# Three more of the zero fills written in rows of 56 KB, in a decode step with its gradients

## The chip, the cores and the metric

The kernel runs on one core of a Trainium2 chip. The metric is device time in microseconds, measured by whole runs; the profile comes from one further execution that the hardware profiler recorded.

## What is computed

One decode step of attention over a cached window, gated by a small dense network, and the gradients of all inputs:

```python
# x: (2, 1, 512); k_cache, v_cache: (2, 8, 32768, 128); wq: (512, 4096); wo: (4096, 512)
W = min(4096, max(256, Sk // 4))                    # 4096
k = repeat(k_cache[:, :, Sk - W:, :], rep); v = repeat(v_cache[:, :, Sk - W:, :], rep)
p = softmax(einsum("bhqd,bhkd->bhqk", q, k) * Dh ** -0.5)
s = einsum("bhqk,bhkd->bhqd", p, v) -> rows @ wo
g = silu((relu(xn @ w1 + b1) ** 2) @ w2 + b2)       # xn = layernorm(x)
out = x + s * g
# returned: out and the gradients by x, k_cache, v_cache, wq, wo, w1, b1, w2, b2
```

Only the last 4096 of the 32,768 cached positions take part. So the gradients by k_cache (out_2) and v_cache (out_3), 134 MB each in bfloat16, are computed in their last eighth and are zero in the other seven eighths. Writing these zeros is most of what the kernel moves: 32 blocks (2 tensors x 2 batch rows x 8 heads) of 28,672 rows of 128 bfloat16 values, 7.34 MB each.

## The kernel before

**The fills.** Each of the 32 blocks of zeros is one "fill". Fills 0 to 30 (the loop at L118 to L123; 0 to 15 go to out_2, 16 to 30 to out_3) are issued at the start of the program by GpSimd, on the software DMA queue; fill 31 comes at the very end from SyncE (L641). The source is the tile `zt` (L80, L81): 128 partitions of 14,336 zero bytes, set once by VectorE. The function `zf` (L90 to L102) issues one DMA: `nent` partitions, each writing `rows` cache rows of 256 bytes in one piece, repeated `rep` times. The source is bytes and the destination is wider, so the DMA widens each byte as it goes: with up to 112 rows (`ZG`) to a piece the destination counts as bfloat16 and 14,336 source bytes become 28,672; above that (L95 to L97) it counts as 32-bit float and the same 14,336 source bytes become 57,344.

There are three forms of fill:

- long (`zlong`, L107): one instruction, 128 pieces of 224 rows, 57,344 bytes (56 KB) each;
- undivided but not long: one instruction, 128 pieces of 112 rows, 28,672 bytes (28 KB), twice. These are fills 0, 1, 9, 14 and 21;
- divided (`zshort`, L108 to L117): fills 2, 4, 6, 8, 10, 13, 15 and 20, in four or five instructions of different piece sizes, down to single rows of 256 bytes.

Together they are 58 instructions. GpSimd may have eight of them outstanding: the first eight start at once and each later one waits until the one eight before it has landed (each of eight semaphores serves every eighth fill). GpSimd does hardly anything else, only one small store in the last round (L512).

**The computation.** It runs in four rounds (L430), each of one batch row and four heads. A round needs the V window and the K window, 4 MB each, which SyncE loads (`load`, L215 to L218) in packets of 32 KB into one buffer for V and one for K. TensorE transposes V in groups and multiplies (`scores`, L378 to L392), then K, then the softmax and its gradient follow on ScalarE and VectorE. `outer_store` (L412 to L422) then writes the gradient by V over the V buffer itself and ScalarE stores it to out_3; only when that store has landed may SyncE load the next round's V (L543). K goes the same way (L548, L550). So within a round the stores and loads of one buffer follow each other strictly, and the transfers share the 16 DMA engines with the fills.

**The end.** In the last round the remaining gradients are computed; ScalarE stores wq's and wo's (L581, L587), SyncE stores w2's (out_8, L610), the gradient by x (L634) and w1's (out_6, L636). Behind these, on SyncE, stands fill 31 (L641), in pieces of 14,336 bytes; it is kept behind the out_6 store and also waits until fill 29, the last but one of the software queue, has landed (L642).

Of the kernel before, what the change touches and what calls it, by code (L numbers as in the profile page):

```python
# [16 lines left out]
def kernel(  # L17
# [86 lines left out]
    ZQ = 2 * B * HKV  # L104
    zparts = [(out_2, q) for q in range(B * HKV)] + [(out_3, q) for q in range(B * HKV)]

    zlong = (3, 5, 7, 11, 12, 16, 17, 18, 19, 22, 23, 24, 25, 26, 27, 28, 29, 30)  # L107
    zshort = {  # L108
        2: ((5, 8, 2), (120, 68, 3), (128, 32, 1), (16, 1, 1)),
        4: ((3, 1, 2), (2, 99, 6), (128, 112, 1), (128, 102, 1), (86, 1, 1)),  # L110
# [561 lines left out]
```

## Time and profile before

| | us |
|---|---|
| median of 3 runs | 766.2 (766.17 to 766.35) |
| the profiled execution | 766.29 |
| its span | 764.5 |
| PE busy | 399.7 (52%) |
| DVE busy | 275.8 (36%) |
| ACT busy | 214.5 (28%) |
| GpSimd busy | 35.1 (5%) |

| moved | |
|---|---|
| written to HBM | 280.50 MB |
| read from HBM | 45.62 MB |
| mean rate over the span | 427 GB/s |
| DMA packets | 12,473 |

The span runs from the first to the last instruction of the program; the execution's own time adds what lies around it. Engines: PE is TensorE's matmuls, DVE VectorE, ACT ScalarE, POOL GpSimd, SP SyncE. A DMA is counted from its issue to its landing; its bytes travel as packets on one of the queues (q0 the software queue, q1 SyncE's, q10 ScalarE's), and all queues share 16 DMA engines. One contiguous piece of a fill is one packet: the records of single packets show 2304 of 57,344 bytes and 2176 of 28,672 on q0. The page shows the span in 40 equal slices; a digit is the busy share of a slice in tenths. The chain of waits is the work that ended last, followed back from the last instruction.

### The profile page before, as it was taken

To read this page: it belongs to the slowest core of one execution; us is meant where nothing else is said; L and a number is where in the kernel's file an instruction comes from. 1 tells how busy PE (TensorE), PEld (TensorE's weight loads), DVE (VectorE), ACT (ScalarE), POOL (GpSimd) and SP (SyncE) were. 2 spreads that over 40 slices of the span, in tenths; PEclk is the share of its full clock that TensorE was granted. 3 is DMA by queue.
4 is the path that set the end of the run, shared out by engine and by line. 5 is a ranking of instruction groups with operands and counts; after the bars stand their busy time and mean duration, and the time that the engine had idled before them with its cause. 6 is when DMAs were issued, how large, how long until landed. Compare 5 with 4: busy or idle time off the path is not lost.

```text
span 764.5 us, 9399 instructions
## 1 busy us (share of the span) xinstructions
PE 399.7 (52%) x4118; PEld 261.8 (34%) x4118; DVE 275.8 (36%) x483; ACT 214.5 (28%) x313; POOL 35.1 (5%) x67
## 2 busy tenths in 40 slices
PE   0166774848503766870486683017645938759100
PEld 0153363734102654430275430016543424232000
DVE  3034252355501346450254653003343515567100
ACT  0034441145500124560122553002142307316100
POOL 3000010010000000000000000000000000000000
PEclk9998898968755995785599577559876957555555
DMA  9999999999999999999999999999999999999998
GB/s 360 433 425 427 442 422 430 438 426 425 429 428 438 427 446 430 413 427 435 435 427 440 427 433 438 420 433 429 437 430 436 430 440 430 418 438 425 436 417 379
DMA packets 12473, 326.73 MB, mean 427 GB/s; under 512 B 2898, under 2 KB 2906, under 8 KB 2934
## 3 DMA queue, kind: packets, MB, share of 16 engines
q0 software_dynamic: 8000, 227.55, 70.4%
q1 hardware_dynamic: 2696, 56.63, 19.3%
q10 hardware_dynamic: 1736, 41.95, 13.5%
q8 instruction: 32, 0.52, 0.3%
q14 instruction: 9, 0.07, 0.0%
HBM read 45.62 MB, written 280.50 MB: 427 GB/s over the span
## 4 chain that ended last, share of the span: by engine, by line
PE 33%; DMA 32%; DVE 14%; ACT 7%; issue 6%; ACTq 0%; DVEq 0%; SPq 0%
DMA out_dram<-nat 13%; DMA nat<-in_A_v_cache_dram 8%; DMA nat<-in_A_k_cache_dram 8%; PE ov L418 5%; PE s_ps L391 4%; PE tp L384 4%; DMA b_bf<-in_B_b_dram 4%; DVE tring L159 3%; PE dp_ps L391 2%; ACT p_bf L452 2%; ACT nat L157 2%; DVE ds_bf L465 2%; DVE nat L159 2%; PE wps L585 2%; PE ps L407 1%
## 5 line engine op out<-in xcount | busy, mean ns | idle before, releaser
L384 PE MATMUL tp<-pperm,nat 128*128 128x128 bf16 x1024 | 81.9, 228 | 136.4 <-DMA nat<-in_A_v_cache_dram 117.3
L159 DVE COPY tring<-tp 128x1024 bf16<-128x1024 bf16 (+1 forms) x98 | 65.5, 689 | 177.9 <-PE tp L384 168.3
L384 PEld LDWEIGHTS <-nat 128*128 128x128 bf16 x1024 | 70.8, 102 | 142.9 <-DMA nat<-in_A_v_cache_dram 119.3
L157 ACT CAST nat<-ov 128x512 bf16<-128x512 f32 x160 | 87.4, 590 | 61.9 <-PE ov L418 61.2
L157 ACT COPY tring<-tp 128x1024 bf16<-128x1024 bf16 (+1 forms) x34 | 34.4, 1011 | 239.7 <-PE tp L384 223.1
L159 DVE CAST nat<-ov 128x512 bf16<-128x512 f32 x96 | 65.7, 690 | 54.1 <-PE ov L418 51.4
L391 PEld LDWEIGHTS <-zz 128*128 128x128 bf16 x512 | 49.6, 100 | 37.3 <-issue 31.3
L101 POOL DMA_DIRECT2D out_dram<-zt x58 | 33.5, 581 | 529.3 <-DMA out_dram<-zt 526.1
L418 PE MATMUL ov<-bd,ds_bf 128*128 128x512 bf16 x128 | 49.2, 459 | 5.6 <-DVE nat L159 3.7
L418 PE MATMUL ov<-bd,p_bf 128*128 128x512 bf16 x128 | 48.6, 452 | 4.3 <-DVE nat L159 1.4
L391 PE MATMUL dp_ps<-tring,zz 128*128 128x256 bf16 x256 | 39.2, 284 | 12.1 <-DVE tring L159 6.9
L391 PE MATMUL s_ps<-tring,zz 128*128 128x256 bf16 x256 | 39.0, 275 | 10.9 <-DVE tring L159 9.9
L407 PE MATMUL ps<-t,nat 128*128 128x16 bf16 x1024 | 29.0, 174 | 13.7 <-DVE bd L372 6.8
L407 PEld LDWEIGHTS <-nat 128*128 128x128 bf16 x1024 | 28.9, 104 | 16.6 <-issue 11.4
L159 DVE CAST wq<-wps 128x512 bf16<-128x512 f32 x16 | 11.0, 690 | 42.4 <-PE wps L578 42.2
L399 PE MATMUL tp<-ident_bf,p_bf 128*128 128x128 bf16 x64 | 7.5, 312 | 34.9 <-ACT p_bf L452 34.9
L452 ACT ACTIVATE p_bf<-e_sb,rl 32x512 bf16<-32x512 f32 x16 | 22.8, 1424 | 3.4 <-DVE rl L449 3.3
L157 ACT CAST wq<-wps 128x512 bf16<-128x512 f32 x16 | 9.3, 586 | 50.6 <-PE wps L578 50.6
L465 DVE SCALAR_TENSOR_TENSOR ds_bf<-dp_ps,delta,p_bf 32x512 bf16<-32x512 f32 x16 | 21.8, 1360 | 0.2
L418 PEld LDWEIGHTS <-ds_bf 128*128 128x128 bf16 x128 | 12.9, 107 | 20.5 <-issue 18.2
L418 PEld LDWEIGHTS <-p_bf 128*128 128x128 bf16 x128 | 12.7, 108 | 19.5 <-issue 16.4
L399 PEld LDWEIGHTS <-p_bf 128*128 128x128 bf16 x64 | 6.5, 145 | 36.0 <-ACT p_bf L452 36.0
(195 smaller groups left out, 437.6 us busy)
## 6 DMA issues: line engine op xcount, KB each, us to landing
out_dram<-zt POOLq DMA_DIRECT2D x23, 7168.0 KB, 101.3
out_dram<-nat ACTq DMA_DIRECT2D x8, 4096.0 KB, 41.4
out_dram<-zt POOLq DMA_DIRECT2D x7, 3584.0 KB, 63.4
nat<-in_A_v_cache_dram SPq DMA_DIRECT2D x4, 4096.0 KB, 32.6
nat<-in_A_k_cache_dram SPq DMA_DIRECT2D x4, 4096.0 KB, 27.3
out_dram<-zt SPq DMA_DIRECT2D x1, 7168.0 KB, 52.2
out_dram<-zt POOLq DMA_DIRECT2D x2, 3488.0 KB, 64.6
out_dram<-zt POOLq DMA_DIRECT2D x1, 6120.0 KB, 85.8
```

The source lines that it names most:

```text
L101: sw_fill.append(nc.gpsimd.dma_start(out=v, in_=zs))
L157: nc.scalar.copy(out=out_ap, in_=in_ap)
L159: nc.vector.tensor_copy(out=out_ap, in_=in_ap)
L384: nc.tensor.transpose(tp[:, j, :], nat[:, g * CC + half * CH + j, :], pperm[:].rearrange("p b k -> p (b k)"))
L391: nc.tensor.matmul(out_ps[:, half * CH * PB:(half + 1) * CH * PB], lhsT=zbuf[:, pr, o:o + R], rhs=tT[:, :, pr, :], start=(g == 0 and pr == ...
L399: nc.tensor.transpose(tp[:, cc, :], src[:, half * CH + cc].rearrange("r k b -> r (k b)"), ident_bf[:, :])
L407: nc.tensor.matmul(ps[:], lhsT=nat[:, g * CC + half * CH + cc, :], rhs=cols[half][:, cc, :, g, :], start=(half == 0 and g == 0 and cc == 0 ...
L418: nc.tensor.matmul(ov[:], lhsT=src[:, cc].rearrange("r k b -> r (k b)"), rhs=bd[:, gh * 4:(gh + 1) * 4, :], start=True, stop=True)
L452: nc.scalar.activation(out=p_bf[rb, :, :, pr], in_=e_sb[rb], func=ACT.Copy, scale=rl[rb, 0:1])
L465: nc.vector.scalar_tensor_tensor(out=ds_bf[rb, :, :, pr], in0=dp_c[rb], scalar=delta[rb, 0:1], in1=p_bf[rb, :, :, pr], op0=ALU.subtract, o ...
L585: nc.tensor.matmul(wps[:], lhsT=o_rows[:, j:N:NJ], rhs=ds_rows[:, :], start=True, stop=True)
```

## The change

Fills 9, 14 and 21 are added to the list of long fills. Their one instruction each then writes 128 pieces of 57,344 bytes in place of twice 128 pieces of 28,672 bytes. The bytes, the number and order of the instructions, the source tile and all waits stay. Fills 0 and 1 keep pieces of 28,672 bytes.

```diff
-    zlong = (3, 5, 7, 11, 12, 16, 17, 18, 19, 22, 23, 24, 25, 26, 27, 28, 29, 30)
+    zlong = (3, 5, 7, 9, 11, 12, 14, 16, 17, 18, 19, 21, 22, 23, 24, 25, 26, 27, 28, 29, 30)
...
     for qi in range(ZQ - 1):
         r = 0
         whole = (P, ZR // P, 1) if qi in zlong else (P, ZG, ZR // (P * ZG))
         for n, rows, rep in zshort.get(qi, (whole,)):
             r = zf(*zparts[qi], r, n, rows, rep)
```

## The prediction, made before the result

> **What bounds the kernel now.** I read the page's slices first, because a kernel that mostly moves bytes shows there whether its transfers or its chain of waits set the end.
>
> ```profile
> DMA  9999999999999999999999999999999999999998
> GB/s 360 433 425 427 442 422 430 438 426 425 429 428 438 427 446 430 413 427 435 435 427 440 427 433 438 420 433 429 437 430 436 430 440 430 418 438 425 436 417 379
> ...
> q0 software_dynamic: 8000, 227.55, 70.4%
> q1 hardware_dynamic: 2696, 56.63, 19.3%
> q10 hardware_dynamic: 1736, 41.95, 13.5%
> ```
>
> The reader is to see that no slice is below nine tenths but the last, and that the rate stays near 430 GB/s whatever the engines compute. q0 is the software queue (the fills), q1 holds SyncE's transfers, q10 ScalarE's. PE is busy for 52% of the span, so it is not the bound. The DMA engines are: 326.73 MB at 430 GB/s need 760 us of the 764.5.
>
> Next the stretches around the fills concerned and at the end (columns: stretch, length, five engines' busy time, clock, DMA share, GB/s):
>
> ```profile
> 530.30:547.10 16.80, 9.95 (x107) 8.51 (x105) 3.71 (x6) 2.02 (x2) 0.54 (x2) 0.80 1.10 454
> 547.10:564.00 16.90, 11.09 (x130) 9.30 (x127) 7.36 (x15) 4.44 (x6) 0.53 (x2) 1.00 1.01 429
> ...
> 711.40:743.40 32.00, 0.00 (x0) 0.00 (x0) 0.00 (x0) 0.00 (x0) 0.00 (x0) 0.50 0.99 423
> 743.40:760.80 17.40, 0.00 (x0) 0.00 (x0) 0.00 (x0) 0.00 (x0) 0.00 (x0) 0.50 1.00 430
> 760.80:764.50 3.70, 0.00 (x0) 0.00 (x0) 0.00 (x0) 0.00 (x0) 0.00 (x0) 0.50 0.37 159
> ```
>
> From 711.4 on nothing computes, and the transfers still need 52 us at full rate. The last row is the only loose end: 0.59 MB in 3.7 us, so the 16 engines do not stop together.
>
> Third, GpSimd in order of time. Each fill instruction waits for the one eight before it (eight start at once, later ones one by one), so its start marks a landing. With fill 9 the 24th fill instruction, fill 14 the 36th and fill 21 the 49th, these rows give the time in which each was moved: fill 9 from 239.5 to 266.1, fill 14 from 363.2 to 384.8, fill 21 from 530.3 to 547.1. Fills 18 and 22 (56 KB rows) are 440.5 to 457.4 and 547.1 to 564.0.
>
> ```profile
> 239.51 0.59 POOL L101 DMA_DIRECT2D out_dram<-zt  x1 [5.83 <-DMA out_dram<-zt]
> 266.05 1.14 POOL L101 DMA_DIRECT2D out_dram<-zt  x2 [25.95 <-DMA out_dram<-zt]
> ...
> 363.18 0.53 POOL L101 DMA_DIRECT2D out_dram<-zt  x1 [14.38 <-DMA out_dram<-zt]
> 384.77 0.53 POOL L101 DMA_DIRECT2D out_dram<-zt  x1 [21.06 <-DMA out_dram<-zt]
> ...
> 440.46 0.55 POOL L101 DMA_DIRECT2D out_dram<-zt  x1 [16.19 <-DMA out_dram<-zt]
> 457.36 0.53 POOL L101 DMA_DIRECT2D out_dram<-zt  x1 [16.35 <-DMA out_dram<-zt]
> ...
> 530.27 0.53 POOL L101 DMA_DIRECT2D out_dram<-zt  x1 [0.93 <-DMA out_dram<-zt]
> 547.07 0.53 POOL L101 DMA_DIRECT2D out_dram<-zt  x1 [16.26 <-DMA out_dram<-zt]
> 563.98 0.53 POOL L101 DMA_DIRECT2D out_dram<-zt  x1 [16.38 <-DMA out_dram<-zt]
> ```
>
> Last, who shares the engines with fill 9. Between 248 and 256 us the DMA view has a load of K (32 KB packets) beside it:
>
> ```profile
> q1 hardware_dynamic: 57, 1.87, 54.8%
> q0 software_dynamic: 55, 1.58, 46.3%
> ```
>
> As many packets of one queue as of the other, so the bytes divide as the packet sizes do.
>
> **What the Trainium skill says.** "DMA: Bandwidth & Descriptors", section "Queues, rings and completion order", says that an engine goes round-robin over the queue rows that have work, a packet at a time. The 57 to 55 above agrees, and a row of a fill counts there as one packet. The same page, "Issuing engines are not separate DMA queues": transfers from all issuers share the same 16 engines; the constant rate agrees. Its section "Where 436 GB/s comes from" puts the ceiling at 435.2 GB/s; the trace holds 429 to 433 over long stretches. "Why small descriptors are slow" names a fixed cost of about three cycles per packet; the packet records here show a few ns (below).
>
> **The change part by part.** 3 fills x 256 rows of 28 KB go, 3 x 128 rows of 56 KB come. The 58 fill instructions, their order, their waits and their bytes stay, and nothing moves on any engine or past any other queue.
>
> (a) *The packets themselves.* In the packet records a 28,672-byte row takes 1.079 us on its engine, a 57,344-byte row 2.153 us: 2 x 1.079 - 2.153 = 0.005 us less for each long row. Each engine gets 384 / 16 = 24 of them: -0.12 us. The landings say the opposite, but little: fill 21 (28 KB rows, almost alone) took 16.80 us, fills 18 and 22 (56 KB rows) 16.90 and 16.91: +0.11 each, +0.33 for three. That interval starts and ends with the engine that is furthest behind, so I trust the records more: I take -0.1 and keep -0.12 to +0.33.
>
> (b) *Loads beside these fills.* A hardware packet of 32 KB now waits for a row of 56 KB: one turn is 1.06 us longer (28,672 B at 27.1 B/ns, the rate of a long fill on one engine: 7.34 MB / 16 / 16.9 us). The K load of round 1 lies inside fill 9 (issued 236.6, landed after 25.8 us, at 262.4). It has 128 / 16 = 8 packets an engine, so it lands up to 8 x 1.06 = 8.5 us later. TensorE reaches its K transposes near 264, so some 1.5 us is free and up to 7 passes to the chain. Fill 14 lies beside the end of round 2's V load and most of its K load (issued 369.5): 118 packets of q1 move there, 7.4 an engine, up to 8 us. Fill 21 now sees only the last packets of round 3's K load, for which TensorE waits 5.03 us at 540.5; if that load comes later, all of it falls there, up to 8.5. Lower end: 2 us in all. Upper: 7 + 8 + 8.5 = 23.5. I take 12.
>
> (c) *What such a delay costs.* Its cover is the fills still queued. While a load or a store is late, its engine time goes to rows of later fills, so the total work and the rate are kept. At the end: of the 13.52 MB in 711.4 to 743.4, 6.48 are fills and 4.26 ScalarE's stores (DMA view of that stretch). Only out_8, out_6 and the last fill (1.84 + 1.84 + 7.34 MB) hang on SyncE's last issues at 704.2, 710.8 and 711.4. So with these late the engines still have 10.74 MB, or 25 us, and another 4 us from out_8, which is issued 7 us ahead. A chain that is 29 us late costs nothing; 12 us costs nothing. The last fill also waits for fill 29's landing (711.3 by its semaphore), which comes earlier, not later, when the chain slips.
>
> (d) *The issue side.* GpSimd's 0.53 us per fill is off the path: the last fill instruction issues at 564 and lands at 742.
>
> Sum: -0.1 + 0 + 0. The profiled execution took 766.29 us, 1.8 more than its span; it stands 0.1 above the median, so the forecast in medians is 766.1.
>
> **The rivals.**
>
> *Slower: the chain slips beyond its cover.* The three fills have 3 x 8 long turns an engine, so 25.4 us at most is lost directly in them. But with a slip, round 3's loads also slide from fill 20 (28 KB rows and 56 short ones) into fills 21 to 23, 8 turns x 1.06 = 8.5 us more. That makes 34, and it decides from 29 on: +5 us, 771. For it: these loads do lie on the chain (the K load's 32.2 us at 508.25 is one of its long pieces). Against it: every packet would have to be hit, and the slack of round 1 counts off. 0.11.
>
> *The loose end grows.* The engines' last packets end between 760.9 and 763.2 us. If the long rows shift which engine is behind by one or two packets of the last fill (0.53 us each), the end moves by 0.5 to 1: 767.1. For it: the end is set by one engine alone. Against it: each engine gets the same share of these rows. 0.14.
>
> *Faster: fewer switches pay.* Fills 9 and 14 move at 431 to 432 GB/s beside loads, the long rows of 564 to 614 at 433. If all 65 us gained that 0.4%, it would be -0.3, and engines that stop together would give 1.0 more: 764.9; two packets beyond that pass the bound. 0.06 for anything below it.
>
> *The rows are cut again.* If a 56 KB row went out as two packets, nothing would change: 766.2. The records of the other long fills show single packets of 57,344 bytes, so I give it nothing apart.
>
> **How the numbers follow.** 0.69 for the forecast, the rest as above (of the loose end 0.03 lies past the bound). What this kernel's measurement tells from no change is put at 0.2%, 1.5 us: 764.7 to 767.7. The forecast and nearly all of the loose end lie inside: 0.80 within, 0.14 slower, 0.06 faster. The range leaves those two out and spans (a) with half a loose end below and a whole one above: 765.2 to 767.6.
>
> **What would show it.** q0 should have 7,616 packets; the K load of round 1 should land 28 to 34 us after its issue; SyncE's last issue should move from 711 to 715 to 735, with the software queue done before 743; the DMA row should stay at nine tenths to the last slice. I am wrong if the DMA share drops after 735 because the last fill is issued too late, if one engine runs on alone at the end, or if the rate inside the three fills falls.

## The result, and the profile after

The changed kernel is slower: 825.3 us median (805.0 to 834.1 in 6 runs) against 766.3 (766.1 to 767.4), a ratio of 1.060 with a 95% interval of 1.053 to 1.068. The ratio leaves out runs more than 1.5% above the fastest of their kernel (three of the six), and the profile below is of such a run, at 834.05 us, with a span of 832.3. Experiment 9 has the profile of a shorter run of nearly the same kernel.

The page's slices of the profile after, with the chain by line:

```profile
DMA  9999999999999999999999999999999994147179
GB/s 360 434 432 419 439 424 445 419 438 422 433 430 429 446 428 428 424 434 438 428 434 428 424 445 426 433 433 421 448 423 437 435 436 189 76 180 303 51 334 397
...
q0 software_dynamic: 7616, 227.55, 64.6%
...
DMA nat<-in_A_k_cache_dram 21%; DMA out_dram<-nat 15%; PE ov L418 5%; PE s_ps L391 4%; DMA b_bf<-in_B_b_dram 4%; PE tp L384 3%; ACT p_bf L452 2%; ACT nat L157 2%; DVE tring L159 2%; DVE ds_bf L465 2%; DVE nat L159 2%; PE wps L585 1%; PE ps L407 1%; PE dops L312 1%
```

The change did what it says: 7616 packets in place of 8000, for the same bytes. Up to slice 33 the engines move as much as before. Then there is a hole: the fills are used up, and the engines wait for the computation. Loads of K stand at 21% of the chain now. Before they stood at 8%:

```profile
DMA out_dram<-nat 13%; DMA nat<-in_A_v_cache_dram 8%; DMA nat<-in_A_k_cache_dram 8%; PE ov L418 5%; PE s_ps L391 4%; PE tp L384 4%; DMA b_bf<-in_B_b_dram 4%; DVE tring L159 3%; PE dp_ps L391 2%; ACT p_bf L452 2%; ACT nat L157 2%; DVE ds_bf L465 2%; DVE nat L159 2%; PE wps L585 2%; PE ps L407 1%
```

The hole in stretches (columns as in the prediction: stretch, length, busy time of five engines, clock, DMA share, GB/s):

```profile
698.00:714.00 16.00, 15.79 (x89) 7.04 (x89) 6.20 (x16) 4.74 (x9) 0.00 (x0) 0.89 0.00 1
714.00:801.00 87.00, 68.73 (x539) 33.41 (x539) 52.79 (x84) 36.79 (x64) 0.50 (x1) 0.59 0.41 176
801.00:809.00 8.00, 6.45 (x16) 1.80 (x14) 4.93 (x9) 4.82 (x9) 0.00 (x0) 0.50 1.00 426
809.00:832.30 23.30, 0.00 (x0) 0.00 (x0) 0.00 (x0) 0.00 (x0) 0.00 (x0) 0.50 0.93 394
```

The software queue has nothing left at 698, where it lasted until 743 before. What follows is paced by the last round's computation, and after its last issue 23 us of transfers remain.

SyncE's issues of the profile after say how late the chain was at each step:

```profile
252.83 0.54 SPq L217 DMA_DIRECT2D nat<-in_A_k_cache_dram  x1
396.86 0.54 SPq L217 DMA_DIRECT2D nat<-in_A_v_cache_dram  x1
428.55 0.54 SPq L217 DMA_DIRECT2D nat<-in_A_k_cache_dram  x1
566.42 0.54 SPq L217 DMA_DIRECT2D nat<-in_A_v_cache_dram  x1
598.09 0.54 SPq L217 DMA_DIRECT2D nat<-in_A_k_cache_dram  x1
...
808.83 0.41 SPq L641 DMA_DIRECT2D out_dram<-zt  x1
```

| SyncE's issue | before | after | late by |
|---|---|---|---|
| K load, round 1 | 236.6 | 252.8 | 16.2 |
| V load, round 2 | 340.1 | 396.9 | 56.8 |
| K load, round 2 | 369.5 | 428.6 | 59.1 |
| V load, round 3 | 483.9 | 566.4 | 82.5 |
| K load, round 3 | 508.2 | 598.1 | 89.9 |
| last fill | 711.4 | 808.8 | 97.4 |

The largest step, from 16 to 57 us, comes with the K load of round 1. The chain of waits after, and TensorE's first K transposes behind it (the time in brackets is the engine's wait):

```profile
212.99 39.76 DMA out_dram<-nat
252.83 49.91 DMA nat<-in_A_k_cache_dram
302.79 1.89 PE tp L384 x16
```

```profile
302.79 1.46 PE L384 MATMUL tp<-pperm,nat 128*128 128x128 bf16 x12 [24.07 <-DMA nat<-in_A_k_cache_dram]
```

The same load before, in the DMA view at its issue (the last figure is us from issue to landing):

```profile
nat<-in_A_k_cache_dram SPq DMA_DIRECT2D x1, 4096.0 KB, 25.8
```

The records of its packets cut the two times into three parts:

| K load of round 1, us | before | after |
|---|---|---|
| issue to first packet | 5.4 | 5.3 |
| first packet to end of last | 19.3 | 27.2 |
| end of last packet to landing | 1.2 | 17.4 |

Which fill stood beside this load, GpSimd's starts after tell. As in the prediction each start marks a landing: fill 9 had landed at 256.4, fill 10 by 283.1, fill 11 at 299.5.

```profile
256.39 1.14 POOL L101 DMA_DIRECT2D out_dram<-zt  x2 [26.29 <-DMA out_dram<-zt]
269.52 0.56 POOL L101 DMA_DIRECT2D out_dram<-zt  x1 [11.99 <-DMA out_dram<-zt]
282.54 1.09 POOL L101 DMA_DIRECT2D out_dram<-zt  x2 [12.46 <-DMA out_dram<-zt]
299.54 0.60 POOL L101 DMA_DIRECT2D out_dram<-zt  x1 [15.91 <-DMA out_dram<-zt]
```

The load's first packet came at 258.2, so in this run it missed the changed fill 9. It stood beside fill 10, in rows of about 28 KB as before, and on fifteen engines it was as quick as before: by the records they had reported by 277.9, 25.0 us after the issue. The sixteenth engine was further on in the queue, in fill 11, which is long in both kernels. There a packet of K and a row of 56 KB took turns, 3.4 us for the two, until 285.3. That is the longer middle part: 7.9 us more, close to the 8.5 that the prediction allowed for longer turns, but beside another fill.

The last part is what the prediction did not have. Its picture is the DMA view of the profile after between 287.4 and 302.2 us:

```profile
q0 software_dynamic: 128, 6.42, 102.1%
q1 hardware_dynamic: 1, 0.00, 6.3%
```

One packet of q1 takes 6.3% of 16 engines for 14.8 us, that is one engine's whole time: a packet of 4 bytes, the load's completion on that sixteenth engine. It starts at 287.4, long after the other engines have reported, and ends at 302.2; meanwhile the fills go on at full rate. In the records these completions mostly take multiples of a fill row: 2.16, 4.27, 6.38, 8.49, 10.6, 12.7 and 14.83 us, one to seven rows of 2.11 us. Before, beside rows of 28 KB, the longest was 6.43 us, at the end of round 3's K load.

The three parts, summed over the six loads of V and K in rounds 1 to 3 (they overlap other transfers, so this is no bill of the 97 us):

| six loads, us | before | after |
|---|---|---|
| issue to first packet | 30.3 | 37.4 |
| first packet to end of last | 129.5 | 169.9 |
| end of last packet to landing | 14.7 | 55.3 |

The stretch from the first packet to the last, in which the turns count, and the held completions each grew by about 40 us.

### The profile page after: what moved, and what is told of

Read it like the earlier page. It is cut to its first block, busy times and chain, and to the rows that moved or that the text cites. A ratio compares the mean times of both kernels' runs of the same rounds, so it can differ in the third digit from the quotient of the medians.

```text
span 832.3 us, 9399 instructions
## 1 busy us (share of the span) xinstructions
PE 413.4 (50%) x4118; PEld 268.0 (32%) x4118; DVE 276.0 (33%) x483; ACT 214.8 (26%) x313; POOL 34.4 (4%) x67
## 2 busy tenths in 40 slices
DMA packets 12089, 326.73 MB, mean 393 GB/s; under 512 B 2898, under 2 KB 2906, under 8 KB 2934
## 3 DMA queue, kind: packets, MB, share of 16 engines
q0 software_dynamic: 7616, 227.55, 64.6%
q1 hardware_dynamic: 2696, 56.63, 19.3%
## 4 chain that ended last, share of the span: by engine, by line
DMA 40%; PE 27%; DVE 12%; another core or an unknown queue 7%; ACT 7%; issue 4%; ACTq 0%; SPq 0%; DVEq 0%
DMA nat<-in_A_k_cache_dram 21%; DMA out_dram<-nat 15%; PE ov L418 5%; PE s_ps L391 4%; DMA b_bf<-in_B_b_dram 4%; PE tp L384 3%; ACT p_bf L452 2%; ACT nat L157 2%; DVE tring L159 2%; DVE ds_bf L465 2%; DVE nat L159 2%; PE wps L585 1%; PE ps L407 1%; PE dops L312 1%
## 5 line engine op out<-in xcount | busy, mean ns | idle before, releaser
L384 PE MATMUL tp<-pperm,nat 128*128 128x128 bf16 x1024 | 86.0, 235 | 232.5 <-DMA nat<-in_A_v_cache_dram 169.6
L384 PEld LDWEIGHTS <-nat 128*128 128x128 bf16 x1024 | 74.4, 106 | 240.4 <-DMA nat<-in_A_v_cache_dram 171.6
L391 PEld LDWEIGHTS <-zz 128*128 128x128 bf16 x512 | 51.2, 103 | 37.6 <-issue 30.3
L391 PE MATMUL s_ps<-tring,zz 128*128 128x256 bf16 x256 | 41.4, 287 | 10.2 <-DVE tring L159 9.0
L407 PEld LDWEIGHTS <-nat 128*128 128x128 bf16 x1024 | 28.6, 103 | 9.8 <-DVE bd L372 5.2
```

The lines of the kernel that those rows point to most:

```text
L384: nc.tensor.transpose(tp[:, j, :], nat[:, g * CC + half * CH + j, :], pperm[:].rearrange("p b k -> p (b k)"))
L391: nc.tensor.matmul(out_ps[:, half * CH * PB:(half + 1) * CH * PB], lhsT=zbuf[:, pr, o:o + R], rhs=tT[:, :, pr, :], start=(g == 0 and pr == ...
L407: nc.tensor.matmul(ps[:], lhsT=nat[:, g * CC + half * CH + cc, :], rhs=cols[half][:, cc, :, g, :], start=(half == 0 and g == 0 and cc == 0 ...
```

## The experiments

### 1 to 3: each fill alone

For fill 9; the other two likewise:

```diff
-    zlong = (3, 5, 7, 11, 12, 16, 17, 18, 19, 22, 23, 24, 25, 26, 27, 28, 29, 30)
+    zlong = (3, 5, 7, 9, 11, 12, 16, 17, 18, 19, 22, 23, 24, 25, 26, 27, 28, 29, 30)
```

> Fill 9 alone in 56 KB rows. Theory A (the chain of loads and stores slips past its cover of some 29 us, and the slip grows because a late chain meets further long fills): fill 9 is the first of the three and hits the stores and the K load of round 1, so it brings most of the loss, 800 us or more, with the last issue of SyncE at 770 us or later. Theory B (each of the three fills costs its own share, some 20 us): about 786 us. Theory C (the packets or the rate of a long fill as such): about 786 us too, but with the last issue of SyncE within 15 us of 711 and a rate below 425 GB/s inside the fill.

> Fill 14 alone. Theory A: rounds 0 and 1 run as before, round 2's loads slip by 10 to 25 us and round 3's a little more; that is about the cover, so 766 to 780 us, with the last issue of SyncE between 725 and 750 us. Theories B and C: about 786 us.

> Fill 21 alone. Theory A: only the end of round 3's K load lies beside it, so the last issue of SyncE slips by at most 10 us, inside the cover: 766.2 us, within 0.2%. Theories B and C: about 786 us.

Fill 9 alone gave four runs at 766.3, 778.6, 793.3 and 794.6 us (the last is the profiled one); fill 14 alone 796.4 us, ratio 1.0387 (1.037 to 1.0405); fill 21 alone 766.3 us, 0.9999 (0.999 to 1.0008). So the loss is no sum of equal shares, as theories B and C have it, but theory A's numbers were off too: fill 9 did not have to bring the most, and fill 14 cost 30 us where 0 to 14 was allowed. SyncE's last issue, with fill 21 alone and then with fill 14 alone:

```profile
735.30 1.15 SPq L641 DMA_DIRECT2D out_dram<-zt  x1
```

```profile
771.12 0.41 SPq L641 DMA_DIRECT2D out_dram<-zt  x1
```

Fill 21 made the chain 24 us late and cost nothing (span 764.4); fill 14 made it 60 us late and cost 30 (span 794.6). Both obey one rule, with the profiled runs of all kernels that keep this last fill: the span is the last issue plus 23.4 us when that issue is after 741, and 764 to 766 otherwise (769.5 only with the plain 14 KB rows of experiment 6). The changed kernel's 808.8 gives 832.2 (832.3 measured), fill 9 alone 769.4 and 792.8. The cover is thus 741 - 711.4 = 30 us; no profiled run has its last issue between 735.3 and 750.8, so the point itself is worked out and not seen. The lateness itself remained to be explained: fill 21 alone had been given 10 us at most.

### 4: the same three fills in 14 KB rows

```diff
+        if qi in (9, 14, 21):
+            whole = (P, ZG // 2, 2 * ZR // (P * ZG))
```

> The same three fills in rows of 14 KB, four times, instead of twice 28 KB. Theory A: loads get more of the engines beside these fills, so the last issue of SyncE comes before 711 us or stays, and the end stays where the total of the bytes puts it: 766.2 to 766.8 us. Theory C, with a cost per packet of a fill: 1536 rows in place of 768 at the 5 ns that the records gave are 0.2 us, so 766.4 us; with a cost that falls with the row's size, a gain of several us.

766.5 us, ratio 1.0001 (0.9993 to 1.001), all 12 runs between 766.4 and 767.1; SyncE's out_6 issue moved from 710.8 to 705.9. As expected: loads do better, the end stays.

### 5: row length or widening

```diff
-    def zf(o, q, r0, nent, rows, rep=1):
+    def zf(o, q, r0, nent, rows, rep=1, wide=False):
...
-        if w > ZG * DH:
+        if wide or w > ZG * DH:
...
-            r = zf(*zparts[qi], r, n, rows, rep)
+            r = zf(*zparts[qi], r, n, rows, rep, qi in (9, 14, 21))
```

> Fills 9, 14 and 21 keep rows of 28 KB, but widen 7 KB of source to them (bytes to 32-bit) in place of 14 KB (bytes to 16-bit). The turn that a hardware packet waits for stays 1.06 us. If a load's 4-byte completion is held by a number of rows (7 at most, as the records show), it is held 7.4 us at most beside these fills and the time is 766.2 us; if it is held by the source bytes that were read ahead (7 x 14 KB), it is held up to 14.8 us beside them, SyncE's last issue moves past 720, and the time lies between 766 and 800 us. If the turn alone counts: 766.2 us with no hold above 3 us.

807.3 us, ratio 1.0525 (1.0506 to 1.0543), though no row of the three fills got longer. This is at the lower end of the interval of the change itself. The completions beside fill 9 were held by up to 10 rows of 28 KB (10.6 us). The time came out above the 800 given, but the branch is clear: longer rows in these three fills are not needed for the loss. (The late loads of rounds 2 and 3 met the 56 KB rows of other fills here too, so this run does not say that a row's length is without effect.) What the change and this kernel have in common is that 1 byte read becomes 4 written, in place of 2.

### 6 to 8: all undivided fills in one form

In all three no long rows are left; the undivided fills are rows of 14 KB copied without widening (1:1), rows of 28 KB from 7 KB of source (1:4), and rows of 14 KB from 7 KB (1:2).

```diff
-    zlong = (3, 5, 7, 11, 12, 16, 17, 18, 19, 22, 23, 24, 25, 26, 27, 28, 29, 30)
+    zlong = ()
```

The 14 KB rows set `whole` as in experiment 4, for every fill; the 1:4 rows set `wide` as in experiment 5, for every undivided fill; the plain rows also have a source of the destination's type:

```diff
-        zs = zt[0:nent * st:st, 0:w].unsqueeze(1).to_broadcast([nent, rep, w])
+        src = zt[:].bitcast(BF16) if plain else zt
+        zs = src[0:nent * st:st, 0:w].unsqueeze(1).to_broadcast([nent, rep, w])
```

> All undivided fills in rows of 14 KB that copy 14 KB of source without widening. A store that is issued beside the fills has so far waited 5 rows more for its first packet than one that runs alone (1.2 us): 6.6 us after its issue beside 28 KB rows, 11.3 to 12 us beside 56 KB rows, each row being made from 14 KB of source. If that lead of the fills is a number of source bytes (some 5 x 14 KB) or a number of rows, it is 5 rows of 0.53 us here, and the first packet comes 3.8 us after the issue; if it is bytes written, 6.6 us or more. No completion is held above 4 us. Time: the chain is early, so the bytes bind, with 368 rows an engine more than without long rows at 5 ns each: 768.8 us; between 767 and 770.

> All undivided fills in rows of 28 KB, each widened from 7 KB of source. Lead counted in source bytes: 10 rows of 1.06 us, so a store's first packet comes 11.3 to 12 us after its issue, as beside 56 KB rows, completions are held up to 14.8 us, and the time is that of a late chain, 785 to 840 us. Lead counted in rows: 5 rows, 6.6 us, no completion held above 7.4 us, 767 us.

> All undivided fills in rows of 14 KB, each widened from 7 KB of source. Lead in source bytes: 10 rows of 0.53 us, first packet 6.5 us after the issue. Lead in rows: 3.8 us. The time tells nothing here: 768 to 770 us in both, by the number of the rows.

A fourth, without long rows and otherwise as before (28 KB from 14 KB):

> No fill in 56 KB rows: the 18 long ones write twice 28 KB. Theory A: holds are 7.4 us at most everywhere, SyncE's last issue comes at or before 711, and the time stays at the total of the bytes, 766.2 to 767.2 us with no run near 795. If the long rows bought anything by themselves: 18 x 128 / 16 = 144 rows an engine at 5 ns are 0.7 us, so 766.9.

The lead of the fills is read most cleanly from the last round's store of the gradient by V, which ScalarE issues while nothing but fills moves in bulk. Its issue and its first packets in the 1:4 kernel (ScalarE in order of time, then the DMA view from the issue on, 660.9 to 672.5, and of 672.5 to 674):

```profile
660.83 0.56 ACTq L422 DMA_DIRECT2D out_dram<-nat  x1
```

```profile
q0 software_dynamic: 188, 4.93, 102.3%
q1 hardware_dynamic: 144, 0.00, 95.8%
```

```profile
q10 hardware_dynamic: 16, 0.52, 82.8%
q0 software_dynamic: 7, 0.20, 32.0%
```

For 11.7 us no packet of q10 appears, though the store is issued; then all 16 engines take its first one together. (The 144 packets of q1 are small stores of SyncE, whose long times fit the same wait.) The same store in all forms, by the packet records:

| fills then in the queue | source bytes to written bytes | issue to first packet, us | less the 1.2 of a store alone |
|---|---|---|---|
| none (changed kernel, 724.3) | - | 1.2 | 0 |
| 14 KB rows, plain | 1:1 | 3.9 | 2.7 |
| 14 KB rows from 7 KB | 1:2 | 6.6 | 5.4 |
| 28 KB rows from 14 KB (no long rows) | 1:2 | 6.6 | 5.4 |
| 28 KB rows from 7 KB | 1:4 | 11.7 | 10.5 |
| 56 KB rows from 14 KB (kernel before) | 1:4 | 11.7 | 10.5 |

This store's wait does not follow the row's length, nor the number of rows, nor the bytes written, but the widening: 2.7, 5.4 and 10.5 us are about 1, 2 and 4 times the time in which an engine writes 70 KB, five pieces of 14 KB. The completions behave alike with a larger number: at most 7 rows when a row is made from 14 KB (14.83 us with 56 KB rows), at most 14 when it is made from 7 KB (14.84 us with 28 KB rows), some 100 KB of source in both.

The Trainium skill has two statements that fit this. "DMA: Bandwidth & Descriptors", section "Two DMAs through the same engine are not ordered", says that the read and the write side of an engine are separate queues. The waits above would follow if the reads of a widened fill, being short, ran far ahead and what was read had to be written first; the page does not say this, and it is inferred here. Its section "Queues, rings and completion order" says that the semaphore increment lands only after every earlier write of that engine, across its queues; a load's completion that is held by fill rows agrees. That the lead is a fixed amount of source data is inferred from the table; the engine's buffer was not seen. Why some engines hold a completion and others report at once in the same load stays open. The full lead was seen only where a store meets nothing but fills: the six loads of rounds 1 to 3, which come while other transfers move, had their first packet after 4.0 to 7.2 us in the 1:4 kernel, and after 4.2 to 6.0 in the kernel before.

The times: 1:1 771.1 us, ratio 1.0062 (1.0047 to 1.0077; 767 to 770 us was expected), 1:2 in 14 KB 767.8 us (expected 768 to 770), no long rows 767.0 us, 1:4 in 28 KB 776.4 us (expected 785 to 840). The fourth kernel had its out_6 issue at 682, 29 us earlier than before, and gained nothing: the bytes bind. The 1:4 kernel's last issue was at 750.8, and 750.8 + 23.4 = 774.2 is its span. That is a late chain, but only 39 us late, though all its 23 undivided fills are widened 1:4. In the changed kernel 21 of them are, and its chain was 97 us late (67 in experiment 9, with 20 of them). What differs otherwise is the row's length, 28 KB and 56 KB. So the length counts as well as the widening.

The 1:1 kernel, the slowest of those with an early chain, ends on a loose end:

```profile
764.00:769.50 5.50, 0.00 (x0) 0.00 (x0) 0.00 (x0) 0.00 (x0) 0.00 (x0) 0.50 0.10 44
```

By the records three engines still have pieces of the last fill after 765.1 us, and one of them runs on to 768.2, where the last packet before ended at 763.2. Why these had more left is open.

### 9: where the runs of the changed kernel part

```diff
-    zlong = (3, 5, 7, 9, 11, 12, 14, 16, 17, 18, 19, 21, 22, 23, 24, 25, 26, 27, 28, 29, 30)
+    zlong = (3, 7, 9, 11, 12, 14, 16, 17, 18, 19, 21, 22, 23, 24, 25, 26, 27, 28, 29, 30)
```

> The changed kernel with fill 5 in rows of 28 KB. If the first K load's completion, held by up to 7 rows of 56 KB of fill 5 in some runs, starts the spread, that load now lands within 3 us of 135, and the runs lie within 12 us of one another, at the lower end: 790 to 810 us. If the spread starts in the later rounds, the runs still spread over 20 us or more around 815.

804.2 us (795.7 to 806.7 in 6 runs), ratio 1.0476 (1.0438 to 1.0513). TensorE's first wait for K in round 0, in the changed kernel and in this one:

```profile
141.80 0.71 PE L384 MATMUL tp<-pperm,nat 128*128 128x128 bf16 x5 [13.64 <-DMA nat<-in_A_k_cache_dram]
```

```profile
134.34 0.72 PE L384 MATMUL tp<-pperm,nat 128*128 128x128 bf16 x5 [7.13 <-DMA nat<-in_A_k_cache_dram]
```

In the kernel before it is 134.1. So up to 7.7 us of the profiled lateness are there before any changed fill is moved: in that run this load's end lies beside fill 5, a long fill of both kernels. With fill 5 shortened the spread of six runs goes from 29 to 11 us, so its form has to do with the longer runs. That this early delay sets a run's length is not shown. The profiled runs of experiment 5 (805.7 us, the fastest of its four) and of fill 14 alone (796.4, with all four runs within 1 us) had the same delay, and so had that of experiment 4, which took 766.65 us:

```profile
142.06 0.71 PE L386 MATMUL tp<-pperm,nat 128*128 128x128 bf16 x5 [15.31 <-DMA nat<-in_A_k_cache_dram]
```

The run of fill 9 alone had it as well (141.8) and issued round 1's K load at 251.0, nearly as late as the changed kernel (252.8). There the load took 26.7 us, and in the changed kernel 49.9, because of its one engine in fill 11. That engine, and not only the early delay, stands behind the length of the profiled run. Single runs of the kernel before, at 795 and 779 us, have no profile, and their cause is open.

This run without the early delay shows the change more plainly. At the six steps of the table above it is late by 6.0, 20.0, 18.0, 50.9, 58.5 and 67.3 us. Round 1's V load, with 86 rows of fill 9 beside it, takes 36.7 us in place of 27.7, with completions held for up to 14.83; round 1's K load takes 30.2. The largest step is round 2's K load, 51.1 us in place of 26.8. It was issued 18 us late and met fills 16 and 17, which are long in both kernels, where before it met fills 14 and 15.

### 10: only these three fills long

```diff
-    zlong = (3, 5, 7, 11, 12, 16, 17, 18, 19, 22, 23, 24, 25, 26, 27, 28, 29, 30)
+    zlong = (9, 14, 21)
```

> Only fills 9, 14 and 21 in 56 KB rows, all other undivided ones in 28 KB rows. Theory A (three transfers lose up to 25 us each beside these fills, and the rest of the slip comes from meeting the other long fills late): the chain without any long row had its last out_6 issue at 682, so even a slip of 50 us stays within the cover (741): 766.8 to 767.5 us. If the three fills cost what they cost in the changed kernel wherever they stand: 805 us or more.

767.0 us, ratio 1.0006 (0.9998 to 1.0015). The changed form of the three fills costs nothing when the other fills are in 28 KB rows: out_6 is issued at 712.8, 31 us later than without any long row (682), and that is within the cover. The rest of the lateness comes with the other long fills, which a late chain meets next. Round 2's K load shows it. In this kernel and in that of experiment 9 it is issued at the same time (SyncE's issue, then the DMA view at that time), here first:

```profile
387.56 0.54 SPq L217 DMA_DIRECT2D nat<-in_A_k_cache_dram  x1
nat<-in_A_k_cache_dram SPq DMA_DIRECT2D x1, 4096.0 KB, 27.8
```

```profile
387.51 0.54 SPq L217 DMA_DIRECT2D nat<-in_A_k_cache_dram  x1
nat<-in_A_k_cache_dram SPq DMA_DIRECT2D x1, 4096.0 KB, 51.1
```

Of the changed fills, 9 and 14 have gone by then and 21 is still to come, in both alike. What differs is the form of the fills beside the load, 16 and 17 above all, and it makes 23 us.

### 11 and 12: the last fill moved to the software queue

```diff
-    for qi in range(ZQ - 1):
+    for qi in range(ZQ):
...
-        fin = nc.sync.dma_start(out=v, in_=zs)
```

> The changed kernel with fill 31 moved from SyncE's end to the end of the software queue (56 KB rows, no wait on fill 29). Theory A (end = last issue of the chain + what still hangs on it): the chain is as late as before, the out_6 store is issued 70 to 97 us after 711, but only its 5 us follow instead of fill 31's 22.5, so each run is some 17 us faster than the changed kernel: 788 to 817 us. Theory of a lower transfer rate: no gain, 805 to 834 us.

> The kernel before with fill 31 moved in the same way. Theory A: the bytes bind, so moving them does nothing: 766.2 to 766.8 us; the cover grows from 29 to some 45 us, so no run near 795 us appears. Theory of a lower transfer rate: the same 766.

With the change 805.3 us (795.1 to 817.0), ratio 1.0382, some 20 us less than the changed kernel; in the profiled run out_6 is issued at 786.6 and only 6.7 us follow. That is theory A's reading of the end. Without the change 769.4 us, ratio 1.0036 (1.0022 to 1.0049), where 766.2 to 766.8 was expected. The stretch from 762.9 us to the end of this kernel:

```profile
762.90:767.80 4.90, 0.00 (x0) 0.00 (x0) 0.00 (x0) 0.00 (x0) 0.00 (x0) 0.50 0.01 3
```

Almost nothing moves there. The last packet ends at 763.8 and the last landing is at 764.6. What lasts longer is GpSimd's closing DRAIN instruction (in its view by line: count, shortest, median and longest in ns, first and last start in us):

```profile
L660 POOLq DRAIN  x3: 40/93/157896, 609.2 to 767.6; - x3
```

The longest began at 609.2 and so ended at 767.1, 3.2 us after the software queue's last packet; the other engines' closing steps follow it. Before it ended 2.9 us after that queue's last packet too, but at 745.9, where it costs nothing. So with the last fill on the software queue these 3 us stand at the end.

No version beat the kernel before: 326.73 MB at 430 GB/s are 760 us, and every kernel with an early chain ends 4 to 10 us above that.

## Why the prediction was wrong

**The bound.** Right. The transfers bind before, and the rate held at 430 GB/s beside a changed fill as well (432 in the stretch of fill 9 after).

**(a) The packets, -0.1 us.** Not contradicted, but too small to tell: without any long row, 144 more rows an engine, the kernel takes 767.0 us against 766.5 measured beside it, a ratio of 1.0006 with an interval of 0.9997 to 1.0015.

**(c) The cover, 29 us.** Right: 30 us. Cost is lateness less cover: 97.4 - 29.7 = 67.7, and the spans differ by 67.8.

**(b) The delay beside these fills, taken as 12 us with 23.5 as its upper end.** This is the step that failed: it was 97 us in the profiled run, and 67 in that of experiment 9. Its mechanism, one turn longer by 1.06 us for each of 8 packets, is real: 7.9 us on the one engine that held round 1's K load. But it counted the wrong transfers, and only this part of each.

- What a late load meets, the largest. The prediction placed each load beside the fill that stood beside it before, and only the slower rival let round 3's loads slide into other long fills, at 8 turns. In fact a load some 20 us late in round 2 falls beside fills 16 to 19, and those of round 3 beside long fills too (25 to 28 in the profiled run). All of these were long before the change too. Experiment 10 shows the size: round 2's K load, equally late, takes 27.8 us beside 28 KB rows and 51.1 beside 56 KB ones, and the three long fills alone make the chain 31 us later than none.
- The held completion, up to 14.8 us. It was put at nothing, and over the six loads it grew by 41 us. The trace of before showed it: TensorE's 5.03 us wait for round 3's K load, which the prediction used, was the tail of a completion held for 6.43 us by six rows of 28 KB. The prediction took it for a load that was merely late.
- The wait for the first packet, the smallest: 7 us more over the six loads. The trace of before showed it at a store: the last round's is issued at 621.2 and has its first packet at 632.8.

Round 1's K load was to land 28 to 34 us after its issue. It took 30.2 in experiment 9's run, which is inside, but the V load before it, which the prediction did not count for fill 9, already took 9 us more.

**The slower rival** was this mechanism with the right threshold (29) and in part the right place, priced at 34 us of lateness by the same step (b), so it came out at 771 and at 0.11. Its bound, that every packet would have to be hit, counted data packets and left the completions out.

**The loose end and the faster rival** fall: nothing shows either in the changed kernel.

**The signs to look for** were chosen well: the DMA share does drop because the last fill is issued too late. But the first hole, at 698 to 714, is there because the software queue has run dry; the prediction put the drop after 735.

## What to carry to other kernels

A background stream that keeps the DMA engines full is free only while the chain of waits has cover, so a change to it is judged by what it does to the latency of the transfers that are waited for: their first packet and their completion as well as their share of the rate. A cover of 30 us is no margin when lateness feeds itself; ask what a transfer meets if it comes 10 us late, and follow that to the end. Beside awaited loads, narrow the widening of a fill and shorten its rows, but only so far as it pays: rows of 28 KB widened 1:2 throughout made the chain 29 us earlier at 767.0 us, and plain rows of 14 KB made it earlier still and ended at 771.1.

## What the runs showed of the hardware

- A store issued while only fills move waits 2.7, 5.4 or 10.5 us longer for its first packet, as the fills copy 1:1, 1:2 or 1:4, whatever the length of a row. At the 27.1 B/ns that one engine writes, that is about 70 KB of source in each case. Loads issued among other transfers waited less.
- The 4-byte completion of a load can be held for up to 14.8 us while its data has long landed, mostly in whole numbers of fill rows (7 of 2.11 us or 14 of 1.06 us).
- The 16 engines do not stand at the same fill: one was in fill 11 while the others were in fill 10, and it alone held a load back by 24 us.
- GpSimd's closing DRAIN ended 2.9 us after the software queue's last packet in the kernel before and 3.2 us after it in experiment 12.
